# Weight chunks in halves, one chunk group moved to an earlier pair, and a new plan, in an attention + two-layer kernel on one core

## The chip, the core and the metric

The kernel runs on 1 core of one Trainium2 chip. The metric is the device time of one execution in microseconds: median of 3 runs of the kernel before. A profiled execution gives the trace; its times are in microseconds from the first instruction, unless marked ns.

## What is computed

Attention with pooled keys and values, then two feed-forward layers, all in float32 with float64 weights given from outside:

```python
B, H, S, D = 8, 8, 576, 64                     # pool = 8, Sp = 72
k_p = k.reshape(B, H, Sp, pool, D).mean(axis=3)
v_p = v.reshape(B, H, Sp, pool, D).mean(axis=3)
scores = scale * q @ k_p.T ; attn = softmax(scores)
x = (attn @ v_p)  ->  [4608, 512]
h = x @ w_in ; g = np.maximum(0.01 * h, h) ; x = g @ w_out            # first layer, d_ff = 2048
h = x @ w_in ; g = h * np.clip(h + 3, 0, 6) / 6 ; out = g @ w_out     # second layer, d_ff = 2048
```

## The kernel before

**Precision.** TensorE multiplies in its 32-bit fast form (`F32R`), and every operand is split in a high and a low part, so that a product is three matmuls (high·high, high·low, low·high). Weights come as 64-bit floats and are decoded on the core: `decode` (L736) is two ScalarE and two VectorE operations over 1024 (a whole chunk) or 512 (half of it) columns, then a copy makes the high part and a subtraction on VectorE the low part.

**Order of the work.** There are 24 attention units (8 batches × 3). The first layer does three tiles of tokens directly (`moe_tile`): tile 0 with 384 tokens on weight chunks 0 to 7, tile 1 with 512 tokens on all 16 chunks, then tile 0's tokens again on chunks 8 to 15. The other tokens of the first layer go in 4 pairs of tiles (`Pair1`), and the second layer in 5 pairs (`Pair`). A pair multiplies by the 2×2 block scheme with 7 products instead of 8. Its weight-side operands, 7 products of each of 8 chunk groups, lie in DRAM (`Left`, tile name `left`): `first_weights` and `pair_weights` make them for the first layer, `second_weights` (L1045) for the second, from `wq` (2 loads of 1 MiB) by `decode`, `combine` (L979) and `split_off` (L958), which writes each product in two pieces of 256 KiB (`left<-st`, L974). Then the pairs stream them back (`stream`, L1116; 512 KiB pieces where `rows` is 2, 1 MiB where it is 4). `Pair.first` has four quarters j of 14 steps; quarter j needs groups 2j and 2j+1. `Pair.second` has 56 steps, all eight groups for each product in turn. While a pair runs, jobs are hung in at steps ("slots", 0 to 55 in `first`, 56 to 111 in `second`; a slot past the last step runs at its end): attention units, preparation of the next pair, and chunk groups (`C["left2"]`: list t of tile or pair t, entries (group, slot)).

**The plan.** `Plan` (L104) collects tasks with an engine, a cost in ns, and the views read and written; `order` puts them in order by a list schedule with these costs, once forward and once backward in 12 rounds, and the kernel issues every engine's instructions in that order. So costs (`SCORES`, `act_cost`, `pe_cost`, `plan.rate` in bytes/ns and `plan.landing` in ns for a DMA) don't change an instruction, but its place. Each DMA is issued by SyncE, in one queue, in order. Where the plan has TensorE idle for over 200 ns before tile 0's second products start, it puts in fill matmuls of zeros (L1576). `copy` (L301) may go to ScalarE or VectorE for the first `C["flex"]` tasks. `plan.sooner` brings the load of some chunks forward.

**The start.** Units 0 and 1 (the first 384 tokens' heads) go first: keys, scores, pooled values on TensorE (`pool_v`), transposes, values (L655), and the split into `xh` and `xl`. Then `gemm1` (L814, matmuls L824 to L826) multiplies by `w_in` and `gemm2` (L852, L861 to L863) by `w_out`. A chunk in `raw` has `w_in` in its first 1024 words and `w_out` in the second; in `wf` the planes 0 and 2 are high and low of `w_in`, 1 and 3 of `w_out`. `weights(f)` (L1453) loads chunk f (1 MiB, L733) and decodes it whole; both `gemm1` and `gemm2` wait for all of it (`wf()`).

**Unsplit attention.** Units of batches under `n32` (`whole32`) keep the transposed attention and the values in plain float32: one matmul of that kind in place of three, and no low parts to subtract.

Of the kernel before, what the change touches and what calls it, by code (L numbers as in the profile page):

```python
# [13 lines left out]
I32 = mybir.dt.int32  # L14
# [15 lines left out]

ROUNDS = 12
C = dict(
    n32=3,
    soon={0: 0, 1: 1000, 2: 0},
    flex=488,
    mid=8,
    when0=[0, 0, 0, 0, 7, 8, 8],
    att0=[1, 4, 10],
    gaps0=[0, 0, 0, 0, 3],
    when1=[6, 13, 20, 26],  # L40
    att1=[0, 7, 16, 25],
    gaps1=[0, 1, 1, 5, 3],
    att2=[0, 3],
    gaps2=[0, 6, 3, 6, 0],
    prep2=[12, 47],
    att=[[0, 25, 40, 60], [6, 21, 39, 54, 77], [0, 24, 46, 57], []],
    gaps=[[0, 5, 5, 10, 0], [0, 5, 9, 12, 1], [0, 5, 9, 10, 7], [3, 10, 0, 14, 3]],
    prep=[[86, 116], [90, 97], [99, 100], [85, 93]],
    left1=[[(0, 48)], [(1, 0), (2, 2), (3, 10)]],
    left2=[[], [], [(0, 50)], [(1, 15), (2, 39)], [(3, 23), (4, 34)], [(5, 32)], [(6, 3), (7, 2)]],  # L50
)
SCORES = 1700
WIDE_SCORES = 1510
EXPS = 1782
TRANSPOSES = 260
FIRST_LOADS = 1.35
# [192 lines left out]
def attention_moe_moe(ctx: ExitStack, tc: tile.TileContext, qt, kt, vm, vr, wt, wq, eye, mask, out):  # L249
# [15 lines left out]
    plan = Plan()  # L265
# [162 lines left out]
    def prep_k(u):  # L428
        held_keys[u.g] = u.b
        if u.early:  # L430
            parts = [(half_k(u, i), part(u.ks, i, lambda t, i=i: t[:, 72 * i : 72 * i + 72]), i, 72) for i in range(2)]
        else:
            parts = [(u.k, u.ks, None, 144)]
        for src, mid_, i, n in parts:
            sum_pool(mid_, src, n)
            for e in range(2):
                r, c = slice(64 * e, 64 * e + 64), slice(SP * e, SP * e + SP)
                src = View(mid_.buf, mid_.key, lambda t, r=r, cut=mid_.cut: cut(t)[r])
                if i is None:
                    src.cut = lambda t, r=r, cut=mid_.cut: cut(t)[r].rearrange("p (a n) -> p a n", a=2)  # L440
                dst = View(keys[u.g].buf, e if i is None else (e, i), lambda t, i=i, r=r, c=c: t[r, :, c] if i is None else t[r, i, c])
                copy(dst, src, n, scale=1.0 / 64.0)

    def prep_v(u):
        if u.b == (1 if u.whole32 else C["n32"]):
# [186 lines left out]
    def values(u, x):  # L632
        assert all(held_values[g] == u.b for g in u.groups)
        pss = []
        columns = u.columns()
        for pi in range(2):
            ps = u.bank("v", pi)
            pss.append(ps)
            groups = []
            for g, c0, n in columns:  # L640
                if u.whole32:
                    ops = [(whole_v[g], u.t[pi])]
                else:
                    th, tl = u.t[pi]
                    vh, vl = [t() for t in vbd[g]]
                    ops = [(vh, th), (vh, tl), (vl, th)]
                ops = [(l, lambda l=l, pi=pi: l.ap()[:, pi, :], r) for l, r in ops]
                r = vrm[g]() if u.b else whole_r[g]
                ops.append((r, lambda r=r, pi=pi: r.ap()[:, 128 * pi : 128 * pi + 128], u.tr))
                groups.append((c0, n, ops))  # L650

            def emit(ps=ps, groups=groups):
                for c0, n, ops in groups:
                    for i, (_, l, r) in enumerate(ops):
                        PE.matmul(  # L655
                            out=ps.get()[:, c0 : c0 + n], lhsT=l(), rhs=r.ap()[:, c0 : c0 + n], start=i == 0, stop=i == len(ops) - 1
                        )

            cost = sum((3.6 * n + 8 if u.whole32 and not u.b else 1.8 * n + pe_cost(n) + 8 if u.whole32 else 4 * pe_cost(n) + 8) for _, n, _ in groups)
            on_pe(cost, emit, [v for _, _, ops in groups for l, _, r in ops for v in (l, r)], [ps()])  # L660
        if u.n == 2:
            both = lambda t: t[:, 0 : 2 * TAIL].rearrange("p (g t) -> p g t", g=2)
            if u.b == 0:
                place_of = lambda pi: [(View(x, (pi, 0), lambda t: t[:, pi : pi + 3 : 2, 0:TAIL], [(pi + 2, 0)]), both, 2 * TAIL)]
            else:
                quarter = lambda t: t.rearrange("p (k t) -> p k t", k=4)
                place_of = lambda pi: [(xa(pi, lambda t: quarter(t)[:, pi : pi + 3 : 2, :]), both, 2 * TAIL)]
        else:
            first, at_, n = {0: (0, 0, HALF), 1: (1, TAIL, T1 - TAIL)}.get(u.b, (None, 0, 0))

            def place_of(pi):
                k, out = 2 * u.g + pi, []
                if first is not None:
                    out.append((x((k, 1), lambda t: t[:, k, at_ : at_ + n]), lambda t: t[:, 0:n], n))
                if n < HALF:
                    out.append((xa(pi, lambda t: t[:, pi * HALF + n : pi * HALF + HALF]), lambda t: t[:, n:HALF], HALF - n))
                return out

        xa = buf("xa", [128, 2 * HALF]) if u.b > 0 else None
        for pi, ps in enumerate(pss):  # L680
            if u.b == 0 and u.n < 2:
                k, src = 2 * u.g + pi, ps(None, lambda t: t[:, 0:HALF])
                hi, lo = [t((k,), lambda t, k=k: t[:, k, 0:HALF]) for t in x]
                copy(hi, src, HALF, True, 0.125)
                on_dve(
                    HALF,
                    lambda src=src, hi=hi, lo=lo: DVE.scalar_tensor_tensor(
                        out=lo.ap(), in0=src.ap(), scalar=0.125, in1=f32(hi.ap()), op0=ALU.mult, op1=ALU.subtract
                    ),
                    [src, hi],  # L690
                    [lo],
                )
                continue
            for dst, src, m in place_of(pi):
                copy(dst, ps(None, src), m, True, 0.125)
        if xa is None:
            return
        if u.n == 2:
            c0, rows, c1 = u.b * S + HALF, slice(0, 4), u.b * S + S
            src = lambda: xa.get().rearrange("p (k t) -> p k t", k=4)  # L700
        else:
            c0, rows, c1 = u.b * S + n, slice(2 * u.g, 2 * u.g + 2), u.b * S + HALF
            src = lambda: pair(xa.get())[:, :, n:HALF]
        on_dma(
            512 * (c1 - c0) * (rows.stop - rows.start),
            lambda: DMA.dma_start(out=x1.get()[:, rows, c0:c1], in_=src()),
            [xa(pi) for pi in range(2)],
            [x1((u.b, u.n))],
        )
# [18 lines left out]

    ORDER = [f + 8 * i for f in range(8) for i in range(2)]

    def load_w(f, raw):
        on_dma(
            1 << 20, lambda: DMA.dma_start(out=raw.get().bitcast(I32), in_=wt[ORDER[f]].bitcast(I32)), [], [raw()]  # L733
        )

    def decode(raw, t, l, half=None):  # L736

# [1 line left out]
        words = lambda: raw.get().bitcast(I32).rearrange("p (a n two) -> p a n two", a=4, two=2)[:, a]  # L739
        cut = lambda v: v.ap() if len(v.ap().shape) == 3 else v.ap().rearrange("p (a n) -> p a n", n=256)  # L740
        bits = lambda v: cut(v).bitcast(I32)
        act = lambda emit, v: on_act(n, emit, [raw()], [v], False, 0.075 * n)

        act(lambda: ACT.mul(out=cut(t), in_=f32(words()[:, :, :, 1]), mul=2.0**-112), t)

# [15 lines left out]
            [t],  # L761
        )

    def decode_w(f, raw, t, l):

        decode(raw, t, l)
        wf = buf(f"w{f}", [128, 4, 512], F32R)
        w[f] = wf
        hi = wf("hi", lambda t: t[:, 0:2].rearrange("p a n -> p (a n)"))
        lo = wf("lo", lambda t: t[:, 2:4].rearrange("p a n -> p (a n)"))  # L770
        copy(hi, t, 1024)
        subtract(lo, t, hi, 1024)
        keep(f, wf)

    def keep(f, wf):
# [30 lines left out]
    def split_x(x32, x, n):  # L806
        for k in range(4):
# [3 lines left out]
            copy(hi, src, n)  # L811
            subtract(lo, src, hi, n)

    def gemm1(f, x, n):  # L814
        xh, xl = x
        ps = buf("h", [128, 512], F32, 2, psum)
# [8 lines left out]
                PE.matmul(out=o, lhsT=hi, rhs=xl.get()[:, k, 0:n], start=False, stop=False)  # L825
                PE.matmul(out=o, lhsT=lo, rhs=xh.get()[:, k, 0:n], start=False, stop=k == 3)  # L826

        on_pe(12 * pe_cost(n), emit, [wf(), *(t((k,)) for t in x for k in range(4))], [ps()])
        return ps

    def leaky(dst, src, n, psum=False):
# [20 lines left out]
    def gemm2(f, g, ys, n, start, stop):  # L852
        gh, gl = g
        wf = w[f]
        for o in range(4):

            def emit(o=o):
                c = slice(o * 128, o * 128 + 128)
                hi, lo = wf.get()[:, 1, c], wf.get()[:, 3, c]
                y = ys[o].get()[:, 0:n]  # L860
                PE.matmul(out=y, lhsT=hi, rhs=gh.ap(), start=start, stop=False)  # L861
                PE.matmul(out=y, lhsT=hi, rhs=gl.ap(), start=False, stop=False)  # L862
                PE.matmul(out=y, lhsT=lo, rhs=gh.ap(), start=False, stop=stop)  # L863

            on_pe(3 * pe_cost(n), emit, [wf(), gh, gl], [ys[o]()])

    class Jobs:

# [584 lines left out]
    def weights(f):  # L1453
# [7 lines left out]
            t, l = [temps[at](i, lambda t, i=i: t[:, 1024 * i : 1024 * i + 1024]) for i in range(2)]  # L1461
        if f in C["soon"]:
            plan.sooner[len(plan.tasks)] = C["soon"][f]
        load_w(f, raw)
        decode_w(f, raw, t, l)

    x = new_x()
    for u in (u0, u1):
# [89 lines left out]
    for p, nxt in zip(pairs, pairs[1:]):  # L1558
        prepare_pair(p.jobs, nxt, (80, 96))
    for p in [*pairs1, *pairs]:  # L1560
        plan.landing, plan.rate = (0, 400) if p in pairs else (900, 340)
        if p in pairs:
            p.new_spare()
        if p is pairs[0]:
# [4 lines left out]
        p.first()  # L1569
        if p is pairs[0]:  # L1570
            p.rows = 4
        p.second(p is pairs[-1])

    idle = psum.tile([128, 512], F32, name="idle", tag="y0", bufs=1)
# [55 lines left out]
```

## Time and profile before

| | |
|---|---|
| median of 3 runs | 1577.18 us (1577.15 to 1578.86) |
| the profiled execution | 1574.66 us, its span 1572.8 us |
| TensorE matmuls busy | 1556.2 us (99%), 7973 recorded |
| weight loads into TensorE | 1384.1 us (88%) |
| VectorE, ScalarE busy | 1191.7 us (76%), 1007.2 us (64%) |
| DMA | 434.66 MB, 276 GB/s mean |

Busy time is the union of instruction times; matmuls overlap one another, so their pace is read from the starts of two successive rows, not from a duration. In a wait, "A <- B" means that an instruction of line or engine A came to run only when B had ended. The granted clock is TensorE's, 1.00 being 2.4 GHz and 0.50 being 1.2 GHz. SPq is SyncE's DMA queue, ACT is ScalarE, DVE is VectorE, PE is TensorE.

### The profile page before, as it was taken

What the parts mean: (1) busy time and instruction counts of PE and PEld (TensorE: products, weight loads), DVE (VectorE), ACT (ScalarE), POOL (GpSimd) and SP (SyncE); (2) the same over time, 40 slices, a digit from 0 to 9 for tenths busy, and PEclk for the clock granted to TensorE, in tenths of its full rate; (3) what the DMA queues carried; (4) which work ended last, traced back from release to release, by engine and by line L of the source; (5) the groups of instructions that cost most, each with busy time, mean ns of one, the idle gap of its engine ahead of it and who ended that gap; (6) DMA issues with size and microseconds to landing.
All of it is one profiled execution on the core that took longest, in us unless ns stands there. A gap on an engine that the chain in (4) does not pass through costs nothing.

```text
span 1572.8 us, 23193 instructions
## 1 busy us (share of the span) xinstructions
PE 1556.2 (99%) x7973; PEld 1384.1 (88%) x7973; DVE 1191.7 (76%) x2092; ACT 1007.2 (64%) x2315; POOL 2.9 (0%) x14
## 2 busy tenths in 40 slices
PE   9999999999999999999999989999999999999999
PEld 7987898988889889888888979988888888888888
DVE  7988997599669877987387869559756946885494
ACT  7888777767777687766556756445645644664454
POOL 0000000000000000000000000000000000000000
PEclk9999999999999999999999999999999999999999
DMA  8998779998989899999868986756866675676564
GB/s 308 341 343 289 267 259 339 326 313 298 331 310 335 272 315 325 328 314 318 294 226 270 368 316 242 272 197 221 290 210 227 239 254 211 228 253 221 208 233 144
DMA packets 139701, 434.66 MB, mean 276 GB/s; under 512 B 14272, under 2 KB 55360, under 8 KB 120384
## 3 DMA queue, kind: packets, MB, share of 16 engines
q1 hardware_dynamic: 139584, 433.18, 79.2%
q8 instruction: 64, 1.05, 0.3%
q14 instruction: 53, 0.43, 0.1%
HBM read 345.57 MB, written 87.56 MB: 275 GB/s over the span
## 4 chain that ended last, share of the span: by engine, by line
PE 88%; DMA 5%; DVE 4%; ACT 2%; issue 0%; SPq 0%; ACTq 0%; DVEq 0%
PE y L1082 41%; PE h L1082 24%; PE a L1082 12%; PE a L655 2%; DMA left<-st 2%; PE a L503 1%; PE h L825 1%; PE h L824 1%; PE h L826 1%; PE y L861 1%; DMA xl<-left 1%; DMA raw<-wq 1%; PE y L863 1%; PE y L862 1%; PE a L604 1%; PE a L515 1%
## 5 line engine op out<-in xcount | busy, mean ns | idle before, releaser
L947 DVE TENSOR_TENSOR w<-y,w 128x464 f32<-128x464 f32 (+1 forms) x124 | 79.1, 638 | 103.1 <-PE y L1082 99.5
L307 ACT ACTIVATE gh<-w 128x464 fp32r<-128x464 f32 (+1 forms) x140 | 82.5, 589 | 69.1 <-PE y L1082 24.6
L1082 PE MATMUL y<-w,xh 128*128 128x464 f32 (+1 forms) x552 | 123.5, 373 | 1.2 <-DMA xh<-left 1.2
L947 DVE TENSOR_TENSOR w<-w 128x464 f32<-128x464 f32 (+1 forms) x184 | 113.0, 635 | 2.0 <-ACT w L835 1.6
L1082 PEld LDWEIGHTS y<-w,xh 128*128 128x128 f32 x552 | 103.0, 188 | 12.9 <-DMA xh<-left 1.5
L1280 DVE SCALAR_TENSOR_TENSOR gl<-w,gh 128x464 fp32r<-128x464 f32 (+1 forms) x140 | 89.0, 636 | 25.2 <-ACT gh L307 24.7
L304 ACT CAST gh<-w 128x464 fp32r<-128x464 f32 x128 | 74.8, 584 | 44.4 <-PE y L1082 19.6
L1082 PE MATMUL y<-w,xl 128*128 128x464 f32 (+1 forms) x408 | 92.6, 376 | 2.8 <-DMA xl<-left 2.8
L314 DVE TENSOR_TENSOR gl<-w,gh 128x464 fp32r<-128x464 f32 x128 | 81.5, 638 | 17.5 <-ACT gh L304 17.2
L1082 PEld LDWEIGHTS y<-w,xl 128*128 128x128 f32 x408 | 76.6, 189 | 12.4 <-DMA xl<-left 3.2
L835 ACT ACTIVATE w<-w 128x464 f32<-128x464 f32 x96 | 56.6, 599 | 45.6 <-DVE w L947 44.9
L1251 ACT ACTIVATE gh<-w,three 128x464 f32<-128x464 f32 (+1 forms) x60 | 40.9, 681 | 66.2 <-DVE w L947 66.2
L314 DVE TENSOR_TENSOR w<-x,w 128x464 fp32r<-128x464 f32 (+1 forms) x96 | 60.3, 636 | 23.9 <-ACT w L304 23.9
L304 ACT COPY w<-y 128x464 f32<-128x464 f32 (+2 forms) x105 | 57.1, 545 | 32.7 <-PE y L1082 32.4
L947 DVE TENSOR_TENSOR w<-h,w 128x464 f32<-128x464 f32 (+1 forms) x52 | 33.2, 639 | 57.0 <-PE h L1082 54.7
L544 ACT ACTIVATE s<-a,mx 128x72 f32<-128x72 f32 x228 | 69.7, 344 | 10.5 <-DVE mx L537 10.3
L314 DVE TENSOR_TENSOR st<-raw,st 128x512 fp32r<-128x512 f32 x88 | 60.1, 687 | 21.0 <-ACT st L304 20.6
L1082 PE MATMUL h<-w,xl 128*128 128x464 f32 (+1 forms) x300 | 70.4, 380 | 1.3 <-DMA xl<-left 1.3
L1082 PE MATMUL y<-gh,raw 128*128 128x464 f32 (+1 forms) x224 | 69.7, 372 | 0.0
L1082 PE MATMUL y<-w,w 128*128 128x464 f32 x288 | 64.8, 375 | 1.1 <-ACT w L304 1.1
L1082 PE MATMUL h<-w,xh 128*128 128x464 f32 (+1 forms) x288 | 64.6, 372 | 0.0
L1082 PEld LDWEIGHTS h<-w,xl 128*128 128x128 f32 x300 | 57.0, 192 | 8.4 <-issue 1.9
(293 smaller groups left out, 4257.1 us busy)
## 6 DMA issues: line engine op xcount, KB each, us to landing
raw<-left SPq DMA_DIRECT2D x60, 1024.0 KB, 4.9
xl<-left SPq DMA_DIRECT2D x90, 512.0 KB, 5.2
left<-st SPq DMA_DIRECT2D x176, 256.0 KB, 5.2
xh<-left SPq DMA_DIRECT2D x86, 512.0 KB, 5.5
w<-left SPq DMA_DIRECT2D x74, 512.0 KB, 5.4
xh<-left SPq DMA_DIRECT2D x33, 1024.0 KB, 4.8
xl<-left SPq DMA_DIRECT2D x25, 1024.0 KB, 4.8
w<-wt SPq DMA_DIRECT2D x16, 1024.0 KB, 8.0
```

The costliest lines, as they stand in the source:

```text
L304: a = lambda: ACT.copy(out=dst.ap(), in_=src.ap())
L307: a = lambda: ACT.mul(out=dst.ap(), in_=src.ap(), mul=scale)
L314: lambda: DVE.tensor_tensor(out=dst.ap(), in0=a.ap(), in1=f32(b.ap()), op=ALU.subtract),
L503: PE.matmul(out=pss[i // 3].get()[:, 2 * SP * (i % 3) : 2 * SP * (i % 3) + 2 * SP], lhsT=u.q.ap()[:, pi * HALF + CQ * c : pi * HALF + CQ * ...
L515: PE.matmul(out=ps.get()[to, (2 * c + pi) * SP : (2 * c + pi) * SP + SP], lhsT=u.q.ap()[rows, pi * HALF + at_ : pi * HALF + at_ + to.stop ...
L544: ACT.activation(out=at()[:, c, h, :], in_=ps.get()[:, o : o + SP], func=AF.Exp, bias=mx.get()[:, c, h : h + 1], accum_out=sm.get()[:, 4 * ...
L655: PE.matmul(out=ps.get()[:, c0 : c0 + n], lhsT=l(), rhs=r.ap()[:, c0 : c0 + n], start=i == 0, stop=i == len(ops) - 1)
L835: lambda: ACT.activation(out=dst.ap(), in_=src.ap(), func=AF.Prelu, alpha=0.01),
L947: on_dve(n, lambda: DVE.tensor_tensor(out=dst.ap(), in0=a.ap(), in1=b.ap(), op=op), [a, b], [dst])
L1082: PE.matmul(out=o, lhsT=l, rhs=r, start=first and i == m == 0, stop=last and i == len(left) - 1 and m == 2, skip_group_check=True,)
L1251: lambda: ACT.activation(out=r.ap(), in_=h.ap(), func=AF.Relu, bias=three.ap()),
L1280: lambda: DVE.scalar_tensor_tensor(out=lo.ap(), in0=v.ap(), scalar=1.0 / 6.0, in1=f32(hi.ap()), op0=ALU.mult, op1=ALU.subtract),
```

## The change

1. `load_w` and `decode_w` get `halves`: for chunks under `C["halves"]` (17, so all chunks that `weights` makes, 0 to 7) the load is two DMAs of 512 KiB and the decoding is done on 512 columns at a time, `w_in` first. `gemm1` waits for half 0 alone, `gemm2` for half 1 (`of_half`).
2. `left2`: the second layer's first pair makes one chunk group, 7, at slot 5 (before: 7 at slot 2 and 6 at slot 3). The last pair of the first layer makes 5 and 6 (before: 5). Groups 0 to 4 stay in their pairs at other slots.
3. In `first` of that pair DMAs are planned with a landing of 1000 ns and 340 bytes/ns, before 0 and 400.
4. `n32` is 4: the units of batch 3 are unsplit too.
5. Planner costs: `SCORES`, `WIDE_SCORES`, copies of keys, unsplit values; and all slots, gaps and `soon` are new.

```diff
-    n32=3,
-    soon={0: 0, 1: 1000, 2: 0},
-    flex=488,
+    n32=4,
+    soon={0: 0, 1: 2000, 2: 4000},
+    flex=575,
     mid=8,
-    when0=[0, 0, 0, 0, 7, 8, 8],
-    att0=[1, 4, 10],
+    halves=17,
+    when0=[0, 0, 1, 0, 5, 4, 7],
+    att0=[0, 3, 10],
...
-    left2=[[], [], [(0, 50)], [(1, 15), (2, 39)], [(3, 23), (4, 34)], [(5, 32)], [(6, 3), (7, 2)]],
+    left2=[[], [], [(0, 42)], [(1, 27), (2, 47)], [(3, 21), (4, 36)], [(5, 36), (6, 59)], [(7, 5)]],
...
-SCORES = 1700
-WIDE_SCORES = 1510
+SCORES = 1600
+WIDE_SCORES = 1400
...
-                copy(dst, src, n, scale=1.0 / 64.0)
+                copy(dst, src, n, scale=1.0 / 64.0, extra=120)
...
-            cost = sum((3.6 * n + 8 if u.whole32 and not u.b else ...
+            cost = sum((4.3 * n + 8 if u.whole32 and not u.b else ...
...
+    def load_w(f, raw, halves=False):
+        for h in range(2) if halves else (None,):
+            cut = lambda t, h=h: t if h is None else t[:, 1024 * h : 1024 * h + 1024]
+            dst = raw(h, cut)
+            on_dma(
+                1 << 20 if h is None else 1 << 19,
+                lambda dst=dst, cut=cut: DMA.dma_start(out=dst.ap().bitcast(I32), in_=cut(wt[ORDER[f]].bitcast(I32))),
...
-        act = lambda emit, v: on_act(n, emit, [raw()], [v], False, 0.075 * n)
+        act = lambda emit, v: on_act(n, emit, [raw(half)], [v], False, 0.075 * n)
...
+    def decode_w(f, raw, t, l, halves=False):
+        for h in range(2) if halves else (None,):
...
+                th, lh = [part(v, h, lambda t, h=h: t[:, 512 * h : 512 * h + 512]) for v in (t, l)]
+                hi, lo, n = *[wf((what, h), lambda t, a=a: t[:, a]) for what, a in (("hi", h), ("lo", 2 + h))], 512
+            decode(raw, th, lh, h)
+            copy(hi, th, n)
+            subtract(lo, th, hi, n)
...
+    def of_half(wf, h):
+        return [wf(("hi", h)), wf(("lo", h))]
...
-        on_pe(12 * pe_cost(n), emit, [wf(), *(t((k,)) for t in x for k in range(4))], [ps()])
+        on_pe(12 * pe_cost(n), emit, [*of_half(wf, 0), *(t((k,)) for t in x for k in range(4))], [ps()])
...
-            on_pe(3 * pe_cost(n), emit, [wf(), gh, gl], [ys[o]()])
+            on_pe(3 * pe_cost(n), emit, [*of_half(wf, 1), gh, gl], [ys[o]()])
...
-        plan.landing, plan.rate = (0, 400) if p in pairs else (900, 340)
+        plan.landing, plan.rate = (1000, 340) if p is pairs[0] else (0, 400) if p in pairs else (900, 340)
...
         if p is pairs[0]:
             p.rows = 4
+            plan.landing, plan.rate = 0, 400
```

## Rows read from the trace of the kernel before

**Rows 1.** Stretches (us): busy PE, PEld, DVE, ACT, POOL; granted clock; DMA share, GB/s.

```profile
36.10:95.00 58.90, 58.23 (x347) 52.29 (x345) 54.93 (x87) 51.36 (x151) 0.00 (x0) 1.00 0.94 337
...
185.00:245.00 60.00, 56.69 (x350) 52.77 (x348) 55.86 (x102) 42.21 (x135) 0.00 (x0) 1.00 0.77 272
245.00:715.00 470.00, 469.51 (x2453) 420.38 (x2454) 376.09 (x679) 341.45 (x885) 0.00 (x0) 1.00 0.92 316
715.00:858.00 143.00, 142.84 (x680) 127.05 (x679) 95.61 (x162) 83.55 (x152) 0.00 (x0) 1.00 0.82 276
858.00:931.00 73.00, 67.72 (x318) 60.99 (x317) 52.64 (x92) 43.68 (x80) 0.00 (x0) 0.95 0.97 347
```

**Rows 2.** What TensorE waited for, 858 to 931 us: total us, times, longest.

```profile
PE y L1082 <- DMA xl<-left: 2.8, 1, 2.8
PE h L1082 <- DMA xl<-left: 1.3, 1, 1.3
PE y L1082 <- DMA xh<-left: 1.2, 1, 1.2
```

**Rows 3.** Timeline of TensorE, 907 to 930 us: start, duration, what [idle before].

```profile
909.55 2.63 PE L1082 MATMUL h<-w,xh 128*128 128x448 f32 x12
915.01 3.69 PE L1082 MATMUL y<-w,xl 128*128 128x448 f32 x12 [2.83 <-DMA xl<-left]
919.98 4.17 PE L1082 MATMUL h<-w,xl 128*128 128x448 f32 x12 [1.28 <-DMA xl<-left]
923.99 2.64 PE L1082 MATMUL h<-w,x 128*128 128x448 f32 x12
```

**Rows 4.** Stretches again, the eight microseconds behind the first long wait.

```profile
916.00:924.00 8.00, 6.72 (x22) 5.54 (x21) 2.41 (x4) 1.87 (x3) 0.00 (x0) 0.57 0.91 311
```

**Rows 5.** Timeline of SyncE's DMA issues, 878 to 914 us.

```profile
878.67 0.79 SPq L974 DMA_DIRECT2D left<-st  x2
879.52 0.47 SPq L1052 DMA_DIRECT2D raw<-wq  x1
...
902.72 6.50 SPq L974 DMA_DIRECT2D left<-st  x5
...
913.75 0.32 SPq L1121 DMA_DIRECT2D xl<-left  x1
```

**Rows 6.** Groups by line and shape, VectorE, 36 to 245 us: busy us, mean ns.

```profile
L749 DVE SCALAR_TENSOR_TENSOR st<-raw,st 128x512 int32<-128x512 int32 x16 | 10.8, 688 | 2.3 <-ACT st L746 2.1
...
L749 DVE SCALAR_TENSOR_TENSOR w<-w,w 128x1024 int32<-128x1024 int32 x3 | 3.7, 1218 | 0.0
```

**Rows 7.** Fill matmuls (tile idle), 9 to 36.1 us: ns min/median/max, first and last.

```profile
L1576 PE MATMUL idle<-zeros x119: 219/219/230, 9.1 to 35.4; 128*128 128x128 bf16 x119
```

**Rows 8.** Timeline of all engines, 30 to 40 us.

```profile
31.56 1.21 ACT L746 ACTIVATE w<-w 128x1024 int32<-128x1024 uint32 x1
...
33.01 2.58 PE L1576 MATMUL idle<-zeros 128*128 128x128 bf16 x43
...
35.25 0.55 DVE L687 SCALAR_TENSOR_TENSOR xl<-y,xh 128x384 fp32r<-128x384 f32 x1
...
36.08 0.42 PE L824 MATMUL h<-xh,w 128*128 128x384 f32 x1
```

**Rows 9.** Timeline of TensorE: values of an unsplit and of a split unit.

```profile
59.87 0.81 PE L655 MATMUL a<-th,vbd 128*128 128x384 f32 x2
...
61.51 0.34 PE L861 MATMUL y<-gh,w 128*128 128x384 f32 x1
...
208.45 0.34 PE L655 MATMUL a<-th,vbd 128*128 128x384 f32 x1
...
209.98 0.34 PE L861 MATMUL y<-gh,w 128*128 128x384 f32 x1
```

**Rows 10.** DMA issues of the whole execution: KB each, median us to landing.

```profile
xl<-left SPq DMA_DIRECT2D x90, 512.0 KB, 5.2
...
w<-wt SPq DMA_DIRECT2D x16, 1024.0 KB, 8.0
```

More of the change, by code (lines that the diff above doesn't have):

```diff
@@ L32 @@
 C = dict(
-    n32=3,
-    soon={0: 0, 1: 1000, 2: 0},
-    flex=488,
+    n32=4,
+    soon={0: 0, 1: 2000, 2: 4000},
+    flex=575,
     mid=8,
-    when0=[0, 0, 0, 0, 7, 8, 8],
-    att0=[1, 4, 10],
[L39 to L42, printed above, removed]
-    att2=[0, 3],
[L44 to L49, printed above, removed]
-    left2=[[], [], [(0, 50)], [(1, 15), (2, 39)], [(3, 23), (4, 34)], [(5, 32)], [(6, 3), (7, 2)]],
-)
-SCORES = 1700
-WIDE_SCORES = 1510
+    halves=17,
+    when0=[0, 0, 1, 0, 5, 4, 7],
+    att0=[0, 3, 10],
+    gaps0=[0, 0, 0, 2, 0],
+    when1=[7, 6, 21, 26],
+    att1=[0, 7, 14, 24],
+    gaps1=[0, 3, 3, 5, 0],
+    att2=[0, 3],
+    gaps2=[0, 3, 3, 6, 0],
+    prep2=[14, 55],
+    att=[[3, 23, 40, 51], [9, 24, 39, 58, 71], [0, 25, 40, 53], []],
+    gaps=[[0, 7, 8, 11, 0], [0, 11, 9, 18, 1], [0, 5, 10, 11, 6], [7, 11, 5, 11, 4]],
+    prep=[[80, 114], [104, 97], [99, 95], [80, 92]],
+    left1=[[(0, 65)], [(1, 1), (2, 7), (3, 11)]],
+    left2=[[], [], [(0, 42)], [(1, 27), (2, 47)], [(3, 21), (4, 36)], [(5, 36), (6, 59)], [(7, 5)]],
+)
+SCORES = 1600
+WIDE_SCORES = 1400
 EXPS = 1782
@@ L657, in emit @@
                         )
-            cost = sum((3.6 * n + 8 if u.whole32 and not u.b else 1.8 * n + pe_cost(n) + 8 if u.whole32 else 4 * pe_cost(n) + 8) for _, n, _ in groups)
+            cost = sum((4.3 * n + 8 if u.whole32 and not u.b else 1.8 * n + pe_cost(n) + 8 if u.whole32 else 4 * pe_cost(n) + 8) for _, n, _ in groups)
             on_pe(cost, emit, [v for _, _, ops in groups for l, _, r in ops for v in (l, r)], [ps()])
@@ L729, in attention_moe_moe @@
     ORDER = [f + 8 * i for f in range(8) for i in range(2)]
[L731 to L734, printed above, removed]
+    def load_w(f, raw, halves=False):
[5 more added lines that the diff above has]
+                lambda dst=dst, cut=cut: DMA.dma_start(out=dst.ap().bitcast(I32), in_=cut(wt[ORDER[f]].bitcast(I32))),
+                [],
+                [dst],
+            )
     def decode(raw, t, l, half=None):
@@ L762, in decode @@
         )
-    def decode_w(f, raw, t, l):
-        decode(raw, t, l)
+    def decode_w(f, raw, t, l, halves=False):
         wf = buf(f"w{f}", [128, 4, 512], F32R)
         w[f] = wf
[L769 to L772, printed above, removed]
+        for h in range(2) if halves else (None,):
+            if h is None:
+                th, lh, n = t, l, 1024
+                hi, lo = [wf(what, lambda t, a=a: t[:, a : a + 2].rearrange("p a n -> p (a n)")) for what, a in (("hi", 0), ("lo", 2))]
+            else:
+                th, lh = [part(v, h, lambda t, h=h: t[:, 512 * h : 512 * h + 512]) for v in (t, l)]
[3 more added lines that the diff above has]
+            subtract(lo, th, hi, n)
         keep(f, wf)
@@ L1463, in weights @@
             plan.sooner[len(plan.tasks)] = C["soon"][f]
-        load_w(f, raw)
-        decode_w(f, raw, t, l)
+        load_w(f, raw, f < C["halves"])
+        decode_w(f, raw, t, l, f < C["halves"])
     x = new_x()
```

## The prediction

> **What bounds the kernel now.** First the stages: a table of busy time by stretch of the span [rows 1]. It shows TensorE busy for nearly the whole of every stretch, so time can only be won where it stands idle, runs at a lower clock, or does work that isn't needed. From 245 to 715 us (the first three pairs of the first layer) it lacks 0.5 of 470 us although the DMA engines are busy at 0.92. Two stretches stand out: 185 to 245 us (the last tile before the pairs, 3.3 us idle) and 858 to 931 us, the first phase of the second layer's first pair: 5.3 us idle, with the DMA engines at 0.97, the fullest of all.
>
> Second, who TensorE waited for [rows 2]: in that last stretch three waits, 2.8, 1.3 and 1.2 us (5.3 together), each for a landing of product chunks (tile `left`) in a stream buffer. Third, the same place in order of time [rows 3]. Two groups of twelve matmuls, from 915.01 and from 919.98, last until 923.99: 8.98 us, where two groups at the pace before (909.55 to the wait: 12 in about 2.45 us) would take 4.9. Of the 4.1 us more, 1.28 are the second wait; the other 2.8 are clock: from 916 to 924 us the granted clock is 0.57 on average [rows 4], which is a mixture of the 1.2 and the 2.4 GHz level, right behind the idle 2.83 us. So these waits cost 5.3 + 2.8 = 8.1 us.
>
> Fourth, why the chunks were late: the SyncE queue, which issues all DMAs in order [rows 5]. A load of raw second-layer weights is issued as late as 879.52; the products made from them (`left<-st`) go out from 902.72 on, five in 6.5 us; the load of the products for the fourth pair of steps is issued only at 913.75, behind them. The last quarter of the phase needs the products of chunks 6 and 7 and starts at 909.55 [rows 3]. The phase makes these two groups itself, 7 first by its slots and then 6, and the second comes too late.
>
> **The change, part by part.**
>
> *One group instead of two in that pair.* The list `left2` now has chunk 6 in the pair before (slot 59) and chunk 7 alone (slot 5). What a group is, from `second_weights`: 8 decode operations, 4 sums and 7 subtractions on VectorE, 19 at 0.69 us (the 512-column row of [rows 6]) = 13.1 us; 2 loads of 1 MiB and 14 writes of 256 KiB = 5.8 MB on the queue. Removed from 858 to 931 us, the 347 GB/s there (73 us, 25.3 MB) become 19.6 MB, 268 GB/s. The group that goes first was writing its products up to 879, just ahead of that load at 879.52 [rows 5], and those were 30 us ahead of their use; so with one group all three waits and the low clock should go: −8.1 us. Bounds: nothing (the waits stay) and −8.1. I take the whole, since the group that stays is the one that wasn't late. That the planner now reckons 1000 ns to each landing and 340 bytes/ns in this phase brings loads forward and is costed at nothing: what hides it is the freed queue.
>
> *The group that moves to the pair before.* From 715 to 858 us VectorE is busy 95.6 of 143 us [rows 1]; 13.1 more leaves 34 free. The DMA engines carry 276 GB/s; 5.8 MB more make 316, which is exactly what the three pairs before it carried, with 0.5 us of waits in 470. Cost 0, under that cover; without it (products late for their own streams, as at 915) up to the same 8.1 us. SyncE gets 16 issues more there, and the streams of that pair queue behind writes that wait for VectorE.
>
> *The start, and the halves.* Up to 36 us TensorE runs 119 fill matmuls from 9 us on [rows 7], at 2.58/43 = 0.06 us each [rows 8] some 7.1 us of nothing. The last 43 stand between the end of the second unit's values at 33.01 and the first weight matmul at 36.08. What is waited for is `x`: its high part on ScalarE stood behind a 1024-column decode (31.56, 1.21 us) of a chunk that isn't needed yet, and the last low part on VectorE only ended at 35.80 [rows 8]. With halves, `gemm1` needs only the first half of a chunk and `gemm2` the second, much later, so half of the decode can leave this place. The shortest way from 33.01 would be high part 0.5, low part 0.55, hand-overs 0.3: a start at 34.4, 1.7 earlier. I take −1.5, nearest to this row; bounds −5 (most of the fill, if the values of the second unit come sooner too: 512 KB fewer stand in front of them in the queue) and +1.5 (a new order that loses as much).
>
> What halves add: a 1024-column decode takes 1.218 us, a 512-column one 0.688 [rows 6]; twice that is 0.158 more, for 3 VectorE operations in each of 8 chunks 3.8 us (ScalarE likewise). What leaves the start comes back later: second halves of two chunks, 6 operations of 0.688 = 4.1 us. In the first tile VectorE is busy 54.9 of 58.9 us, 4.0 free [rows 1]. So 7.9 against 4.0, bounds 0 and +3.9. I take 0: part of it falls before 36 us, ScalarE has 7.5 us free in the same row and the copies may go to either engine, and preparation of later units can slide into the next tile.
>
> *Batch 3 unsplit (`n32` 4).* Values with unsplit fp32 operands take 61.51 − 59.87 = 1.64 us a unit, with split ones 209.98 − 208.45 = 1.53 [rows 9]: +0.11 for each of three units, +0.3 on TensorE. VectorE loses the three units' six subtractions of the transposed attention, in or near the stretch 185 to 245 us, where it is busy 55.9 of 60. I leave the 3.3 us that TensorE idles there: bounds −3 and +3, taken as 0, since all the order before 858 us is made anew by the planner.
>
> *Two DMAs for one.* Eight more issues on a queue that isn't the bound in this tile: 0. The nearest rows: a 1 MiB load of these weights lands 8.0 us after issue, 512 KiB pieces 5.2 [rows 10]. Two in a row would be 2.4 more than one; overlapped, nothing. The stretch 858 to 931, whose transfers are mostly pieces of 256 and 512 KiB, moved 347 GB/s, more than the 337 of the first tile with its 1 MiB loads [rows 1], so I take nothing.
>
> The Trainium skill says the contrary ("DMA: Bandwidth & Descriptors", under Bandwidth): batch DMAs to 1 MiB or more for 75% of peak. By its fixed 2.0 us per DMA the eight extra ones would be 16 us, an estimate, where my sum has 0; the two rates just named don't bear it out in this kernel.
>
> *Changed costs in the planner* (scores, values, key copies) only reorder; they add no instruction.
>
> **Sum.** −8.1 − 1.5 + 0.3 = −9.3 us against the profiled execution's 1574.66 (span 1572.8 and 1.9 around it): 1565.4. The median of the timed runs stands 2.5 above that execution, so in their terms 1577.18 − 9.3 = 1567.9.
>
> **Rivals.**
>
> *The waits only move.* Chunk 6's writes hold up the streams of the pair before, or chunk 7 alone is still late. For it: one queue, and a write at its head waits for VectorE. Against it: three pairs in front run at that DMA load almost without a wait. Only the start's gain is left: 1577.18 − 1.5 + 0.3 = 1576.0, no change. 0.12.
>
> *VectorE becomes the bound of the first tile.* 3.9 us of waits there: 1567.9 + 3.9 = 1571.8. For it: 93% busy now. Against it: ScalarE's room. 0.09.
>
> *Slower: half loads starve the first tile.* The place is SyncE's queue and the DMA engines from 36 to 95 us, 0.94 busy [rows 1], 3.5 us free. If the 2.4 us more per chunk [rows 10] were occupancy and not latency, 8 × 2.4 = 19.2, less 3.5, would be 15.7 us of TensorE waiting for weights: 1567.9 + 15.7 = 1583.6. It decides for slower only from 12.5 us of waits on, that is if nearly all of the 2.4 is real. Against it: the two rates above. 0.07.
>
> This is what the rule of the Trainium skill named above ("DMA: Bandwidth & Descriptors", Bandwidth) would do here.
>
> **How the numbers follow.** My forecast has 0.72, the rivals 0.12, 0.09 and 0.07. Predicted time 1567.9. Its own range is 1563 to 1572; with the low bound of the start (−3.5 more, and some of the idle at 185 to 245) it begins at 1562.5, and it reaches to 1575 to take in the second rival and part of the first. A measurement here can tell about 0.2%, 3.2 us: faster is below 1574.0. Faster 0.79 (forecast and nearly all of the second rival), same 0.14, slower 0.07.
>
> **What would show it.** Right: in the first phase of the second layer's first pair no TensorE wait over 0.5 us, granted clock 1.00 throughout, DMA share well below 0.97, and the phase about 8 us shorter; the pair before with the DMA near 0.92 and no waits; the first weight matmul at 34 to 35 us with fewer than 119 fills. Wrong: waits for `left` landings in the pair before or after; the first weight matmul later than 36; waits for `w` from VectorE or for weight loads between 36 and 95 us.

## The result, and the profile after

The changed kernel takes 1560.13 us (median of 4 runs, 1557.06 to 1563.06), the kernel before 1578.02 in the same comparison (4 runs, 1577.15 to 1580.13). The ratio is 0.9884, 95% interval [0.9859, 0.9910]: 17.9 us faster by the medians, where 10.1 were forecast against this median (9.3 by the sum). It is under the range, which began at 1562.5. The profiled execution took 1563.06 us, its span is 1561.3.

The stretches of the changed kernel come first, cut at its own stages; columns as in [rows 1].

```profile
9.00:25.80 16.80, 16.50 (x177) 13.47 (x174) 13.61 (x32) 14.93 (x64) 0.00 (x0) 1.00 0.94 349
25.80:36.10 10.30, 10.30 (x54) 5.89 (x46) 7.38 (x16) 8.12 (x33) 0.00 (x0) 0.50 0.76 270
36.10:95.00 58.90, 58.74 (x350) 52.75 (x350) 54.70 (x102) 52.72 (x166) 0.00 (x0) 1.00 0.92 331
185.00:241.00 56.00, 55.06 (x333) 51.38 (x334) 53.49 (x96) 40.35 (x122) 0.62 (x2) 1.00 0.84 297
241.00:711.00 470.00, 469.86 (x2460) 420.23 (x2460) 375.37 (x677) 343.67 (x896) 0.00 (x0) 1.00 0.92 315
711.00:856.00 145.00, 145.00 (x691) 129.29 (x690) 107.71 (x185) 91.86 (x168) 0.00 (x0) 1.00 0.90 310
856.00:923.00 67.00, 67.00 (x332) 61.95 (x331) 44.75 (x79) 39.32 (x70) 0.00 (x0) 1.00 0.93 326
```

The last row is the phase that stood out before: no idle time, clock 1.00. The row above it is the pair that took the moved group: VectorE 107.7 us where it was 95.6, DMA 310 GB/s where it was 276, TensorE without a gap. The second row is new and bad: 10.3 us at the low clock, 1.2 GHz, ahead of the first weight matmul.

What TensorE waited for, over the whole execution (total us, times, longest), no longer has a `left` landing in it, against [rows 2]:

```profile
PE a L605 <- DVE sb L579: 1.8, 1, 1.8
PE idle L1592 <- DVE three L1464: 1.0, 1, 1.0
PE a L656 <- ACT th L305: 0.7, 1, 0.7
PE y L877 <- DVE gl L315: 0.4, 1, 0.4
PE a L516 <- DVE xl L688: 0.3, 1, 0.3
```

The timeline of TensorE in the last quarter of that phase, against [rows 3], goes on at 2.43 to 2.45 us per twelve matmuls:

```profile
905.48 2.61 PE L1097 MATMUL h<-w,xh 128*128 128x448 f32 x12
907.93 2.60 PE L1097 MATMUL y<-w,xl 128*128 128x448 f32 x12
910.36 2.59 PE L1097 MATMUL h<-w,xl 128*128 128x448 f32 x12
912.79 2.59 PE L1097 MATMUL a<-w,x 128*128 128x448 f32 x12
```

The start, again TensorE's timeline (values of the second unit, fill, first weight matmul), against [rows 8]:

```profile
26.65 1.49 PE L656 MATMUL y<-w 128*128 128x384 f32 x2
...
31.22 1.64 PE L656 MATMUL y<-tr,w 32*128 32x384 f32 x2
32.80 3.27 PE L1592 MATMUL idle<-zeros 128*128 128x128 bf16 x29
35.83 0.54 PE L839 MATMUL h<-xh,w 128*128 128x384 f32 x1
```

The values begin at 26.65, 3 us sooner than in the kernel before (they end there at 33.01, after 3.3 us), but take 6.15 us at the low clock, and the 29 fills take 3.0. So in this execution the first weight matmul comes at 35.83, hardly sooner than 36.08. Of the four runs, those at 1557.1 and 1558.1 us have a mean clock of 0.999, those at 1562.2 and 1563.1 have 0.996 and 0.997: the time goes with the clock.

To compare kernels I split the span at three matmuls that can be found in each trace: the first weight matmul (`gemm1`), and, counting the matmuls of the seven-product pairs (6048 in all), the 2689th, with which the second layer begins, and the 3025th, 336 further, one phase. What follows the 3025th lasts 637.8 to 639.0 us in all kernels.

| kernel | first weight matmul at, us | from there to the second layer | the phase of 336 | low clock, us |
|---|---|---|---|---|
| before | 36.08 | 820.6 | 77.1 | 6.8 |
| changed | 35.83 | 818.5 | 68.2 | 10.2 |
| changed, again (a2) | 31.61 | 818.4 | 68.2 | 3.4 |

In the third row the low clock came later, and the start is as it is at the full clock: 4.5 us sooner than before's. The stretch of that execution with its low clock, 3.4 us long:

```profile
44.00:48.00 4.00, 4.00 (x17) 3.95 (x17) 2.30 (x4) 2.67 (x7) 0.00 (x0) 0.57 0.86 318
```

The second and the third row are the same program: the low clock in the start cost 4.2 us (35.83 for 31.61), and the spans of these two executions, 1561.3 and 1557.0 us, differ by 4.3. The 15.8 us between the spans of before's profiled execution and of the one in the third row (1558.73 us, the fastest of its four) are 4.5 at the start, 2.2 in the long middle and 8.9 in the phase, with 0.2 in the rest.

### The profile page after: what moved, and what is told of

Same layout as the page of the kernel before. It is cut to its first block, busy times and chain, and to the rows that moved or that the text cites. A ratio compares the mean times of both kernels' runs of the same rounds, so it can differ in the third digit from the quotient of the medians.

```text
span 1561.3 us, 23152 instructions
## 1 busy us (share of the span) xinstructions
PE 1553.1 (99%) x7924; PEld 1381.6 (88%) x7924; DVE 1188.8 (76%) x2107; ACT 1010.5 (65%) x2338; POOL 2.9 (0%) x14
## 4 chain that ended last, share of the span: by engine, by line
PE 85%; DVE 7%; DMA 3%; ACT 3%; issue 1%; SPq 0%; DVEq 0%; ACTq 0%
PE y L1097 43%; PE h L1097 23%; PE a L1097 13%; PE a L656 2%; DVE raw L962 1%; DVE w L315 1%; DMA left<-st 1%; PE a L504 1%; DMA x<-x 1%; DVE gl L315 1%; PE idle L1592 1%; ACT sb L545 1%; DVE st L315 1%; DMA x<-xa 1%; PE a L605 1%
## 5 line engine op out<-in xcount | busy, mean ns | idle before, releaser
L315 DVE TENSOR_TENSOR st<-raw,st 128x512 fp32r<-128x512 f32 x88 | 59.8, 684 | 17.9 <-ACT st L305 17.6
L308 ACT ACTIVATE sb<-w 128x464 fp32r<-128x464 f32 (+1 forms) x70 | 41.3, 591 | 35.8 <-DVE s L1295 16.5
```

The lines of the kernel that those rows point to most:

```text
L308: a = lambda: ACT.mul(out=dst.ap(), in_=src.ap(), mul=scale)
L315: lambda: DVE.tensor_tensor(out=dst.ap(), in0=a.ap(), in1=f32(b.ap()), op=ALU.subtract),
```

## The experiments

The theory after the result: the moved group gives its 8 us as forecast; the rest, 9.6 us where 1.2 were forecast, comes from the start and from the new order up to the second layer. The rivals: for the first, that the planned landing does it, or that the waits move; for the second, that one part (halves, unsplit batch 3, the costs, VectorE's load) carries it, against slots fitted to one another.

### The phase in the second layer's first pair

**p1_group_moved.** In the kernel before:

```diff
-    left2=[..., [(5, 32)], [(6, 3), (7, 2)]],
+    left2=[..., [(5, 32), (6, 59)], [(7, 5)]],
```

> Before with group 6 alone moved to the pair before (slot 59; group 7 at slot 5). If the two groups in the second layer's first pair were the cause, its three waits of 5.3 us and the low clock behind them go, and the time is 8 to 9 us under before's. If the waits only move, the pair before shows waits on left landings and the time stays within 2 us of before's. If it needs the new landing times in the plan, about half stays.

1568.48 us (before 1576.78), ratio 0.9944 [0.9929, 0.9959]: 8.3 us by the medians. TensorE has no wait at all from 715 to 931 us. The pair that makes the group and the phase that is rid of it:

```profile
715.00:858.00 143.00, 143.00 (x679) 126.65 (x678) 104.11 (x179) 89.84 (x165) 0.00 (x0) 1.00 0.92 315
858.00:924.00 66.00, 66.00 (x327) 61.05 (x326) 42.84 (x75) 37.71 (x68) 0.00 (x0) 1.00 0.89 316
```

315 GB/s where the prediction had 316, and it hides there as the prediction said.

**p2_landing.** In the kernel before, both groups kept:

```diff
-        plan.landing, plan.rate = (0, 400) if p in pairs else (900, 340)
+        plan.landing, plan.rate = (1000, 340) if p is pairs[0] else (0, 400) if p in pairs else (900, 340)
...
             p.rows = 4
+            plan.landing, plan.rate = 0, 400
```

> Before with the planned landing of 1000 ns and 340 bytes/ns in that phase alone, both groups kept in it. If the moved group is the cause, the waits stay: within 2 us of before. If the planned landing alone does it, 6 to 9 us under before.

1576.47 us, ratio 0.9993 [0.9980, 1.0007]: nothing. The waits of the phase are there, at other places (total us, times, longest, 856 to 935 us):

```profile
PE h L1082 <- DMA xl<-left: 2.9, 2, 2.3
PE y L1082 <- ACT w L304: 2.1, 1, 2.1
PE y L1082 <- DMA xh<-left: 1.3, 2, 1.0
```

**p3_two_groups.** In the changed kernel, groups 7 and 6 back in this pair, the planned landing kept:

```diff
-    left2=[..., [(5, 36), (6, 59)], [(7, 5)]],
+    left2=[..., [(5, 36)], [(6, 3), (7, 2)]],
```

> The changed kernel with groups 7 and 6 back in the second layer's first pair (planned landing kept). If the group is the cause, the phase from 856 us on is 6 to 9 us longer again, with waits on left landings in its last quarter; if the planned landing suffices, it is as the changed kernel.

1567.16 us, ratio 0.9941 [0.9925, 0.9958]. The phase takes 77.0 us again, with these waits:

```profile
PE h L1097 <- DMA xl<-left: 2.5, 1, 2.5
PE y L1097 <- DMA xh<-left: 1.7, 2, 1.5
PE y L1097 <- ACT w L305: 1.7, 1, 1.7
```

In all profiles of this study the phase is 68.1 to 68.9 us with one group and 77.0 to 80.9 with two. The group is the cause. This kernel is also the whole change without it: 9.6 us under before by the medians.

### The clock in the start

**f1_fills.** In the changed kernel's `order`, six more fills before each task that the plan has on TensorE between 18 and 26 us:

```diff
                 out += [self.fill] * int((self.starts[i] - busy - 200) / 56)
+                if 18000 < self.starts[i] < 26000:
+                    out += [self.fill] * 6
```

> The changed kernel with 36 more fill matmuls (2 us), six before each of six tasks between 18 and 26 us. In the changed kernel's profile the granted clock is 0.5 for 10.24 us from 25.8 on. If idle places in the fill plan let it fall, the clock now stays at 1.00 in every run, the first weight matmul starts at 32 to 33 us, not 35.8, and all runs lie within 2 us of each other at about 1559. If the clock falls for another cause, the profile still shows it and the runs spread over 5 us, 2 us above the changed kernel's.

In the traces these tasks are eight, not six: 196 fills here and 172 in f2_fewer_fills below, where the changed kernel has 148. So 48 and 24 were added, some 2.7 and 1.4 us, where the expectations say 36 and 18.

```profile
L1592 PE MATMUL idle<-zeros x148: 219/219/314, 1.0 to 35.8; 128*128 128x128 bf16 x148
L1594 PE MATMUL idle<-zeros x172: 219/219/314, 1.0 to 31.6; 128*128 128x128 bf16 x172
```

1558.35 us (1557.27 to 1559.12), ratio 0.9883 [0.9867, 0.9900]; the first weight matmul at 33.16, no low clock before the end, mean clock 1.000 in all four runs. In the trace of the changed kernel no fill stands between 13 and 32.8 us; that its want of fills let the clock fall was the theory, and it fits: with them the low clock is gone, while the order of everything else is the same.

**a2_changed_again** and **f2_fewer_fills** (`* 3` in place of `* 6`), beside each other on one chip.

> The changed kernel again. If its spread is the clock in the start, a run with the clock near 1.00 is at 1557 to 1558 with the first weight matmul at 30.5 to 31.5 us in a profile, and one with 10 us at the low clock is 5 us above; if not, the time doesn't go with the clock.

> Three fills instead of six before each of the six tasks (18, 1 us). If fewer already keep the clock: all runs at 1556.5 to 1558.5 with clock 1.00, up to 1 us under f1_fills. If not, the low clock is back in some runs and they spread over 3 us or more.

The changed kernel again: 1560.08 us, runs at 1558.7 and 1559.7 with mean clock 0.999, 1560.5 with 0.997, 1562.1 with 0.996. The time goes with the clock again, though no run here is below 1558 and the start, at 31.61, is just outside what was expected. TensorE's timeline of its start at the full clock:

```profile
26.74 0.81 PE L656 MATMUL y<-w 128*128 128x384 f32 x2
...
30.00 1.79 PE L1592 MATMUL idle<-zeros 128*128 128x128 bf16 x29
31.61 0.42 PE L839 MATMUL h<-xh,w 128*128 128x384 f32 x1
```

Values that begin at the same place as in the first profile end at 30.00, not 32.80. With f2_fewer_fills' 24 fills: 1556.67 us (1555.18 to 1557.52), ratio 0.9865 [0.9837, 0.9893], clock 1.000 in every run, the first weight matmul at 31.65, no later than the changed kernel's at the full clock. Its median is 3.4 us under the changed kernel's, measured beside it, and its slowest run is under the other's fastest: the best of all kernels here. The stretch that was at 0.50 in the changed kernel:

```profile
25.80:36.00 10.20, 10.20 (x87) 7.90 (x84) 9.69 (x20) 9.97 (x38) 0.00 (x0) 1.00 0.95 347
```

### What brings the start forward

**h1_halves_alone.** The kernel before with the halves of the change, and its own slots, costs and groups:

```diff
     mid=8,
+    halves=17,
```

> Before with the halves alone, its slots, costs and groups kept. If halves bring the start forward by themselves, the first weight matmul comes at 33 to 34.5 us, not 36.1, and the time is 1.5 to 3 us under before's. If the first tile's VectorE is the limit, the earlier start is given back by 140 us and the time is before's or up to 4 us above.

1578.58 us, ratio 0.9994 [0.9981, 1.0007]: no change. But the first weight matmul is at 30.68, 5.4 us sooner, more than expected. TensorE's timeline, with the pooling of the second unit's values (the 16 matmuls at 16.85), its values, and the first weight matmul:

```profile
16.85 1.95 PE L417 MATMUL h<-w,ident 128*128 128x128 f32 x16
18.64 0.81 PE L656 MATMUL a<-w 128*128 128x384 f32 x2
...
25.61 0.91 PE L656 MATMUL y<-w 128*128 128x384 f32 x2
...
28.97 1.90 PE L1591 MATMUL idle<-zeros 128*128 128x128 bf16 x31
30.68 0.42 PE L839 MATMUL h<-xh,w 128*128 128x384 f32 x1
```

In the kernel before, that pooling stands behind the first unit's values:

```profile
25.77 3.06 PE L416 MATMUL h<-w,ident 128*128 128x128 f32 x32
```

The queue has the likely cause: the load of the second unit's values (`w<-vm`) is issued at 10.24 in the kernel before, behind two loads of 1 MiB of weights:

```profile
7.41 0.33 SPq L733 DMA_DIRECT2D w<-wt  x1
8.17 0.33 SPq L321 DMA_DIRECT2D w<-qt  x1
8.99 0.33 SPq L733 DMA_DIRECT2D w<-wt  x1
10.24 0.33 SPq L321 DMA_DIRECT2D w<-vm  x1
```

With the halves it is issued at 7.17, ahead of them:

```profile
7.17 0.35 SPq L322 DMA_DIRECT2D w<-vm  x1
7.88 1.06 SPq L738 DMA_DIRECT2D w<-wt  x2
```

No run moved this load alone, but among the kernels without added fills, at the full clock, the start goes with its landing. It lands at 12.2 to 15.3 us in this kernel, a2_changed_again, p3_two_groups and nh_unsplit_halves, which start at 30.7 to 31.6; it lands at 19.1 to 19.9 in the kernel before, p1_group_moved, p2_landing and n1_unsplit_alone, which start at 35.1 to 36.1.

From the first weight matmul to the second layer this kernel then takes 825.9 us, 5.3 more than before; 3.4 us at the low clock, from 43.5 us on, are at most 1.7 of them. What was won is given back; why is not shown.

**h0_whole_chunks.** In f1_fills, `halves=17` to `halves=0`.

> The kernel with the extra fills (f1_fills: 1558.4, first weight matmul at 33.2 us in its profile), chunks loaded and decoded whole again. If the halves make the earlier start, the first weight matmul is 2 to 3 us later and the time 1560.5 to 1562. If the start and what follows come from the plan's costs and slots, it stays within 1 us; if the operations that halves add cost more than they save, it is faster.

1562.83 us, ratio 0.9893 [0.9871, 0.9916], 4.5 over f1_fills; first weight matmul at 34.96, 1.8 later, and 819.3 us behind it, 3.9 more. The first is about what the halves were expected to cost, the second was not expected. The load of the second unit's values is issued as early as in f1_fills (6.70 for 6.59), but behind one load of 1 MiB, and lands at 16.1 us for 13.4: so the halves are not alone in bringing it forward. f1_fills and the kernels that are compared with it ran on several chips, on which the kernel before had medians of 1576.8 to 1579.4 us, so 2 to 3 us between the medians of two of them is not told apart; the two profiles here, both at a clock of 1.000, have spans 5.1 us apart.

### The long middle: parts or slots

**n3_split_batch3.** In f1_fills, `n32=4` to `n32=3`.

> The kernel with the extra fills, batch 3 split again as before (n32 3). If VectorE's missing subtractions are what shortened the stretch up to the first layer's pairs, the first product step starts 2 to 4 us later and the time is 1560.5 to 1562.5; if not, 0.3 us faster by TensorE's own work, 1558.

1572.45 us, ratio 0.9959 [0.9942, 0.9976]: 14.1 over f1_fills, far above both. TensorE's longest waits from 185 to 250 us, where f1_fills has none:

```profile
PE y L1099 <- DVE st L964: 3.4, 1, 3.4
PE h L842 <- DMA xl<-xsl: 1.9, 1, 1.9
PE y L1099 <- ACT w L307: 0.6, 1, 0.6
```

The first waits for VectorE's preparation of the first pair, which fits a VectorE bound; the next two runs test that.

**v1_vector_work** and its control **a1_scalar_work.** In f1_fills, six results that nothing uses, made in batch 3:

```diff
                 copy(dst, src, HALF, True)
+                if u.b == 3:
+                    subtract(buf("tl", [128, HALF], F32R, 2)(), src, dst, HALF)
                 continue
```

> The kernel with the extra fills, batch 3 unsplit, but its six low-part subtractions on VectorE (0.55 us each, 3.3 in all) still made and used by nothing. If VectorE's work sets the time up to the first layer's pairs, 3 us or more over f1_fills: 1561.5 to 1566. If n32 pays by something else (fewer matmuls, operands, buffers), within 1 us of 1558.4.

The control copies `src` to the same place by a ScalarE copy.

> The control: the same six results, used by nothing, copied on ScalarE (0.48 us each). If VectorE alone is the limit there, within 1 us of f1_fills at 1558.4; if any added work or any other order costs as much, as v1_vector_work.

1563.76 us, ratio 0.9905 [0.9881, 0.9929], and 1562.26, ratio 0.9897 [0.9869, 0.9925]: 5.4 and 3.9 over. The control moved nearly as much as the test. And in both the first weight matmul moved, to 36.29 and 36.20, 3 us later, though the added work only comes from 188 us on: that part is the order, made anew, with the load of the second unit's values issued at 10.80 and 7.97 us for 6.59. From the first weight matmul to the first pair, the stretch with the added work, f1_fills takes 201.0 us, the test 201.9, the control 201.3 and n3_split_batch3 211.5. So VectorE's six subtractions by themselves show as 0.9 us there, where n3_split_batch3 loses 10.5.

**c0_old_costs.** In f1_fills, the costs of before (`SCORES` 1700, `WIDE_SCORES` 1510, 3.6 for unsplit values, no extra for keys).

> The kernel with the extra fills, planned with the old costs of scores, unsplit values and key copies; all slots as in the change. If the traced costs are what the gain up to 860 us comes from, half of it or more is lost: 1562 to 1566. If they only relabel, within 1.5 us of 1558.4.

1563.57 us, ratio 0.9905 [0.9882, 0.9927], 5.2 over. As expected of costs that matter; but see the nulls.

**q1_one_slot** and **q2_exp_cost.** In f1_fills, one change each that changes no work:

```diff
-    att1=[0, 7, 14, 24],
+    att1=[0, 7, 14, 25],
```

```diff
-EXPS = 1782
+EXPS = 1790
```

> A null: the kernel with the extra fills, one attention unit hung in one slot later in tile 1 (24 to 25). Same work. If each part's price can be read from a kernel with that part changed, this stays within 1 us of f1_fills at 1558.4; if the slots are fitted to one another, any new order costs 2 to 6 us, and the 4 to 5 us of whole chunks, old costs and added work say no more than that.

> A second null: the planned cost of the exponentials 1790 ns for 1782, nothing else. As q1_one_slot: within 1 us of 1558.4 if parts can be read one by one, 2 to 6 us over if any new order costs that.

1562.22 us, ratio 0.9903 [0.9880, 0.9926], and 1566.38, ratio 0.9932 [0.9908, 0.9955]: 3.9 and 8.0 over f1_fills. One slot, or 8 ns in a planned cost of 1782, costs as much as a part. What TensorE waits for from 36 to 860 us in the second null (the three longest of five):

```profile
PE a L658 <- ACT tr L307: 1.3, 1, 1.3
PE a L607 <- DVE s L581: 1.0, 1, 1.0
PE y L879 <- DVE gl L317: 0.9, 1, 0.9
```

and all that f1_fills has there:

```profile
PE a L658 <- ACT th L307: 0.6, 1, 0.6
PE a L607 <- DVE sb L581: 0.5, 1, 0.5
PE a L629 <- ACT th L307: 0.2, 1, 0.2
```

Small waits for VectorE and ScalarE, none with a place of its own. All five come to 4.6 us for 1.3, which is 3.3 of the 8.2 us more that the second null takes from the first weight matmul to the second layer; the rest is in no wait of the profile.

**n1_unsplit_alone** (the kernel before with `n32=4`) and **nh_unsplit_halves** (with the halves too).

> Before with n32 4 alone. If VectorE's work counts also in the old plan, 3 to 6 us under before's: 1571 to 1576, with the first product step before 239 us (241.2 in before). If it pays only with the new slots, within 2 us of before's.

> Before with n32 4 and the halves, old slots, costs and groups. If the start's gain of the halves was given back for want of VectorE's time, it now stays: 6 to 10 us under before's, more than either alone. If not, the sum of the two alone, which is n1's.

1577.36 us, ratio 0.9997 [0.9982, 1.0013], and 1578.44, ratio 1.0003 [0.9988, 1.0019]. Neither part, nor both, pays in the old slots: nh starts its weight matmuls at 31.02 and needs 825.8 us from there. Its phase with two groups is also the longest of all, 80.9 us.

**o1_old_slots.** f1_fills with the slots, gaps, `soon` and `flex` of before (group 6 moved). **s1_new_slots.** f1_fills with whole chunks, `n32=3` and the old costs.

> All parts of the change and the extra fills, but the slots and gaps of before (with group 6 moved). If the parts carry the gain, 1558 to 1561; if the slots do, only the moved group's 8 us are left: 1568 to 1571.

> The slots and groups of the change and the extra fills, with none of the other parts: whole chunks, batch 3 split, old costs. If the slots carry the gain, 1558 to 1562; if the parts do, 1568 to 1571; if the slots are fitted to these parts, above that, as n3_split_batch3 (1572).

1563.55 us, ratio 0.9919 [0.9895, 0.9944], and 1573.46, ratio 0.9980 [0.9966, 0.9993]. Neither as either theory had it. All parts in old slots lose 5.2 against f1_fills, no more than a null, and the new slots with none of the parts lose 15.1.

The middle and the start, kernel by kernel:

| kernel | us | first weight matmul | to the second layer |
|---|---|---|---|
| f2_fewer_fills | 1556.67 | 31.65 | 817.1 |
| f1_fills | 1558.35 | 33.16 | 815.4 |
| q1_one_slot | 1562.22 | 33.91 | 820.5 |
| q2_exp_cost | 1566.38 | 32.69 | 823.6 |
| a1_scalar_work | 1562.26 | 36.20 | 817.2 |
| v1_vector_work | 1563.76 | 36.29 | 818.8 |
| c0_old_costs | 1563.57 | 33.07 | 821.0 |
| h0_whole_chunks | 1562.83 | 34.96 | 819.3 |
| o1_old_slots | 1563.55 | 34.12 | 820.6 |
| n3_split_batch3 | 1572.45 | 35.09 | 828.7 |
| s1_new_slots | 1573.46 | 40.70 | 822.9 |
| p3_two_groups | 1567.16 | 31.64 | 818.4 |
| p1_group_moved | 1568.48 | 35.14 | 822.8 |
| n1_unsplit_alone | 1577.36 | 35.23 | 822.7 |
| h1_halves_alone | 1578.58 | 30.68 | 825.9 |
| nh_unsplit_halves | 1578.44 | 31.02 | 825.8 |

From f1_fills to the second null the sum of both columns spreads by 8 us (848.5 to 856.3), and n3_split_batch3 stands at 863.8, outside that; the other kernels with one part of f1_fills changed (h0, c0, v1, a1) stand inside, at 853.4 to 855.1.

## Why the prediction was right, and where it was wrong

*What bounds the kernel, and the phase at 858 us: right.* The term was −8.1; the phase became 8.9 us shorter, and the moved group by itself gave 8.3 by the medians. That the planned landing is worth nothing was right too (0.9993 [0.9980, 1.0007]). Around the term some readings were off. The last load of raw weights in the kernel before is issued at 888.97 us, not at 879.52, the second group's products go out from 893.11 on, and two of the first group's fourteen writes come at 885.56 and 889.36. In the changed kernel the one group's writes go out until 908.48, though the last quarter starts at 905.48; so the 30 us of margin were not there, and still no wait came. The DMA engines carry 326 GB/s at a share of 0.93 where 268 and "well below 0.97" were forecast.

*The group in the pair before: right.* No wait there, 310 GB/s and 0.90, against 316 and "near 0.92".

*The start: the term was mis-sized, and this is the step that failed.* The prediction took −1.5 "nearest to this row", from the shortest way behind the values' end at 33.01. That held the end of the values fixed. It is the values that came sooner: the pooling of the second unit went in front of the first unit's values, and at the full clock the second unit's values ended at 30.00, with the first weight matmul at 31.61. That is −4.5 near the outer bound of −5 (−5.4 with the halves alone, beyond it). The likely cause is the one that was given for the bound: their input's load passed the weight loads in the queue (issued at 7.17 instead of 10.24 with the halves alone). The clock in the start was not thought of at all: in the profiled execution the low clock took the gain back (35.83, and 75 fills from 9 us on for 119), and whether it does differs by run. So the sign "34 to 35 us" came out in neither profile.

*The order up to the second layer: taken as 0, between −3 and +3; measured −2.2* (820.6 to 818.4), inside the bounds and on the side that was not taken. The two kernels with fills, whose order is the same, stand at 817.1 and 815.4, −3.5 and −5.2, beyond the bound, so this term is not known to better than some 3 us. Start and order together are −6.7 where the sum had −1.2; that is 5.5 of the 6.5 us missed in the traces (−15.8 for −9.3). The medians moved 17.9 by one comparison and 17.1 by the other, since before's timed runs stand above its profiled one, by 3.4 us here rather than the 2.5 that the prediction added.

*Batch 3 unsplit: unsettled.* The +0.3 can't be seen among changes of this size. Leaving batch 3 unsplit gave nothing alone in the old plan and cost 14.1 when taken out of the new one, more than the nulls' 8.0, so the new slots lean on it; why by so much was not found. VectorE's work alone is not it: made again with nothing else changed, it shows as 0.9 us up to the pairs.

*Two DMAs for one, and VectorE in the first tile: right that neither shows.* Ten of the sixteen half loads are issued before 36.1 us, and from 9 to 25.8 us the DMA engines carry 349 GB/s; from 36.1 to 95 us their share is 0.92 at 331 GB/s, and VectorE is busy 54.7 of 58.9 us, as before. TensorE has no wait at all there, for a weight load or for VectorE; its longest wait for VectorE in this execution, 1.8 us, ends at 185.5 us. The rivals did not come.

What stays open: how much of the middle belongs to which part. The nulls say that a kernel with one part changed cannot tell it below some 4 to 8 us, because the planner then makes another order. The place in the queue is the likely cause of the earlier start, not a tested one.

## What to carry to other kernels

When a stage waits for operands that it makes itself, count what the issuing queue and the vector engines do in that stage and in the one before; a unit of work moved one stage ahead, into a place whose neighbours already run at that load, is a gain that a trace can price well. When a planner makes the order, price a part only after a null has been run: change one slot or one cost by nothing that matters and see how far the time moves. Where a start is bound by a chain of loads, ask which load stands in front of which in the queue, not only how the chain ends.

## What was not expected of the hardware

The mean granted clock of the changed kernel differed between executions of one program, 0.996 to 0.999, and its time with it, 1557.1 to 1563.1 us. The low level came in the start for 10.24 us in one profile and for 3.4 us, 18 us later, in the other. The kernel before spreads in the same way, 0.995 to 1.000 and 1572.8 to 1583.0 us over its runs here, so part of the distance between two medians can be the clock. With 24 fill matmuls more (some 1.4 us) between 18 and 27 us it stayed at 1.000 in all four runs, and the kernel was 3.4 us faster at the median: the fills paid for themselves.
